# First 290 steps of a fused attention and mixer kernel in another order, with every copy of q and k on VectorE or ScalarE

## The chip, the core and the metric

The kernel runs on one core of a Trainium2 chip. The metric is device time in microseconds (us), from one launch to its end; the median of three runs is given. Engines are named as the profile names them: PE is TensorE (matrix products), DVE is VectorE, ACT is ScalarE, POOL is GpSimd, SP is SyncE. Each engine works through its own list of instructions strictly in order. It stops at an instruction whose inputs or whose output buffer another engine has not released yet, and everything behind it waits too.

## The reference, cut to what matters

Attention over 8 batches, 8 heads, 576 tokens and 64 numbers a head, with 16 extra "beacon" keys in front that every token may see; then a mixer over the 512 numbers of each token.

```python
k_all = np.concatenate([beacon_k, k], axis=2)
v_all = np.concatenate([beacon_v, v], axis=2)
scores = scale * np.matmul(q, k_all.transpose(0, 1, 3, 2))
scores = np.where(causal, -1000000000.0, scores)
a = np.exp(scores - scores.max(-1, keepdims=True))
a /= a.sum(-1, keepdims=True) + 1e-09
x = np.matmul(a, v_all)                  # then heads side by side: (8, 576, 512)
...
h = x.transpose(0, 2, 1) @ U @ V         # rank 32 over tokens
u = x + h.transpose(0, 2, 1)
out = u + np.maximum(u @ w_ch1, 0.0) @ w_ch2
```

## The kernel before

The work is cut into **pairs**: pair p holds two heads of one batch, so pairs 0 to 3 are batch 0, pairs 4 to 7 batch 1, and so on to 31. The mixer is cut into nine **blocks** of 512 rows. Nothing schedules itself: one long string, `SCRIPT` (from line 853), names the steps in the order in which they are written into all engines' lists. A step is a short name:

- `kqbv` and a batch: loads of k, q, beacon keys and v, issued from POOL (a letter A or B takes half of the heads). `w10` to `w13`, `w20`, `w21`: loads of the mixer's weights, from POOL too. `u`: small loads from SP for U and V. The first batch's q and k come ahead of the string, a pair at a time: pair 0's q from ACT's queue and everything else from SP's (k0, k1, q1, k2, q2, k3, q3, each a large transfer and a small one with the first 80 rows, "heads", tile `sth`).
- `GqA0`: the **regrouping** of q (or k) of pair 0 on engine A (ACT; V is DVE, G is POOL), from tile `stm` or `st` into `pr` (line 253). For batch 0 this is a cast from 32 to 16 bits, and a second cast brings the heads from `sth` to `hd` (line 741; `H` does that alone).
- `TqA0`: PE turns q of pair 0 (five transposes into the bank `tps`, lines 261 and 263), and engine A copies the result to `qT` or `kT` (two instructions: line 109 on ACT, lines 264 and 265 on DVE).
- `Sa0` to `Sd0`: the four **score visits** of pair 0: PE products `sps` (line 316), and two exponentials on ACT from `sps` to `expt` (line 321). `:3` puts three filler products ahead.
- `M0.0`: DVE masks the scores of one head (lines 304 and 306). `A0.0`: PE multiplies them with v (`po`, line 331), DVE divides by the sums (lines 339 and 340).
- `X0.0`, `X0.1`, `X0.2`: the mixer's rank-32 part for batch 0 (lines 371, 390, 397), with copies to `uT` on ACT (line 408) and DVE (line 406).
- `g0.9`: one of 16 first products of block 0 (four matmuls, line 529), with its relu on ACT (line 539), or ACT and DVE (lines 533 and 534). `p`, `P`: sums and second products of a block (lines 601, 620). `U`, `R`, `x`: transposes by DMA from SP's queue. `W`: sums of weights on DVE.
- `c`, `s`, `e`: three casts of the small loads (lines 163, 164), four copies on DVE (line 159), two products copied by ACT (line 170).
- `B` fills a tile for the masks on DVE. `I1` is a **filler**: one 128x512 product whose result nobody reads (line 241). It keeps PE at work while data are on their way.

There are two kinds of buffers that bind the order: eight PSUM banks, taken in turn by all products, and four score tiles (`expt_120` to `expt_123`), two for each pair, so that pair p+2 waits for pair p.

POOL's queue is served by a limited number of loads at a time: each load waits until the eighth one before it has landed.

Of the kernel before, what the change touches and what calls it, by code (L numbers as in the profile page):

```python
# [27 lines left out]
def kernel(  # L28
# [760 lines left out]
    def step(t):  # L789
# [65 lines left out]
        I1 Sb0 I1 I1 I1 TqV1 Sd0 q1A Sc0 I1 M0.0 GkV3 I1 I1 Sa1:2 I1 GqV2 I1 Sb1 M0.1 I1 I1 GkG2 I1 TkA2  # L855
        TqV2 TkA4 I1 q1B I1 w10 v0B w12 GqA4 I1 Sc1 A0.0 TkV3 Sd1 GqV3 I1 A0.1 Sd2 Sb2 Sa2:1 I1 Sc2 M1.1
        s M1.0 TqV3 GkG5 I1 A1.1 A1.0 Sc3 GqV6 Sa3:1 M2.1 I1 cG I1 I1 GqV5 k1B Sb3 TqV6 I1 Sd3 TqA4 w13
        M2.0 eA k2 M3.1 M3.0 I1 TqA5 A2.1 A2.0 Sc4 Sa4 TkV5 I1 A3.1 GqA7 I1 I1 A3.0 Sd5 Sc5 GkV7 TqV7
        X0.0 Sd4 GkA6 I1 X0.2 X0.1 I1 U0.0 Sa5:0 v1A Sb4 Sb5 g0.8 TkA7 GkV9 M5.1 M4.1 GkV11 M4.0 g0.1
        M5.0 g0.15 g0.0 b2 TkA6 U0.1 GkV8 g0.10 q2 A5.1 A5.0 Sb7 Sa7 Sd7 w11 A4.1 A4.0 g0.11 GqV9 g0.3  # L860
        Sc7 GqV8 M7.1 M7.0 g0.12 Sb6 Sd6 TqV8 TkV9 TkV11 TqV9 g0.2 Sa6:0 GqA11 Sc6 M6.0 v1B g0.14 g0.5
        M6.1 g0.6 g0.9 A6.0 A7.1 A7.0 TkA8 A6.1 w20 g0.13 p00.0 w21 g0.4 Sc9 Sd8 X1.0 g0.7 p01.0 X1.2
        X1.1 p01.1 P01.0 GkV10 p00.1 W0 Sd9 U1.1 TqA11 Sb9 Sa8 W4 W5 W1 P02.0 W2 W3 U0.2 v2 W6 P01.1
# [5 lines left out]
        Sc12 p11.0 GqV15 X2.0 M12.0 P11.0 GkA17 P11.1 U1.2 X2.1 GkV16 p11.1 R15 P12.0 P12.1 R16 P16.0
        TqV14 Sd13 Sb13 M12.1 p10.1 p10.2 Sc13 P16.1 b5 U2.2 M13.0 TkA14 v3 A12.1 q5 A12.0 R17 GkA19  # L870
        P15.0 P15.1 p11.2 Sa14 Sd14 Sc14 x12 P17.0 TkV15 M13.1 P13.0 U2.3 A13.0 Sb14 Z16 M14.0 P17.1
        P13.1 GqA19 GqA18 TkV16 TqA16 A13.1 g2.13 g2.10 TqV17 TqV15 M14.1 v4 g2.4 Sa15 k5 Sc15 TkA17
        P14.0 A14.0 P14.1 A14.1 Sd16 GqV20 Sb15 Sd15 M15.1 GkV18 g2.0 x14 Sc16 M15.0 g2.7 g2.5 g2.2
        A15.0 A15.1 x13 Sd17 Sb17 g2.9 U2.0 X3.0 b6 Sa16 X2.2 g2.3 x15 Sa17 Sb16 R18 R19 Z18 GkV20 M16.1
        Sc17 M17.1 M17.0 g2.1 g2.6 g2.12 M16.0 g2.8 g2.15 A17.0 U2.1 TqA19 GqA21 TqA18 X3.1 A16.1 A17.1
        g2.14 A16.0 X3.2 g2.11 p21.0 P21.0 P21.1 GqA23 GkA21 q6 TkA18 p20.0 P22.0 P22.1 TkA19 R20 p21.1
        p20.1 Sc18 Sb18 P26.0 P26.1 R21 Sc19 Sd18 Sa19 p21.2 P25.0 P25.1 GkV22 p20.2 I1 Sd19 Sa18 M18.0
        U3.0 Sb19 M19.0 P27.0 M18.1 M19.1 P23.0 GqV24 GqA22 TqV20 P27.1 x16 P23.1 g3.11 TqA21 GkV23
        TkV20 TkA21 R22 b7 A19.1 g3.7 A19.0 R23 g3.13 g3.8 g3.5 Sa21 Sb21 Sc21 P24.0 P24.1 A18.1 A18.0
        Sb20 U3.3 Sd21 Sa20 M21.1 M21.0 g3.3 g3.2 Sc20 Sd20 X4.0 g3.4 M20.0 k6 GkV24 M20.1 g3.15 GqA26  # L880
        N5 v5 TkV22 g3.12 A21.0 U3.1 A20.0 g3.10 N1 GkA26 g3.1 x17 q7 g3.0 A20.1 TqV22 TqA23 TkV23 g3.6
        g3.14 g3.9 p30.0 p30.2 A21.1 Sc23 GkV25 p31.0 Sb23 GqV25 Sa23 R24 p30.1 x18 P31.0 P31.1 GkV27
        P32.0 P32.1 TkA24 p31.1 Sc22 p31.2 U3.2 k7 Sd22 v6 Sa22 P36.0 P36.1 Sb22 x19 M22.1 Sd23 M23.0
        P35.0 R25 R26 M22.0 P35.1 X4.1 P37.0 P37.1 X4.2 GqV27 TqA24 TqA25 P33.0 U4.1 P33.1 TkA25 P34.0
        R27 g4.0 GqV28 A22.1 TkV26 GkA28 R28 M23.1 g4.11 GqV29 g4.2 g4.6 TqV26 A23.0 g4.10 A23.1 Sd25
        Sc25 A22.0 g4.4 GkV29 R29 Sb25 GkV30 Sa25 M25.0 Sd24 TqV27 P34.1 TkA27 g4.3 U4.3 TkV28 M25.1
        g4.15 g4.13 g4.9 Sc24 Sa24 x21 Sb24 M24.0 U4.2 X5.0 A25.0 M24.1 g4.8 g4.12 U4.0 GqV31 x22 g4.1
        p40.0 p40.1 GqA30 A25.1 g4.7 Sa27 Sb27 A24.1 g4.14 A24.0 g4.5 p41.0 GkV31 Sc27 x23 Sc26 p41.2
# [140 lines left out]
```

## Time and profile before

| | |
|---|---|
| median of three runs | 341.4 us (340.95 to 341.75) |
| the profiled execution | 341.91 us, its span from the first to the last instruction 340.3 us |
| instructions in it | 8963 |
| DVE, ACT, POOL busy | 263.4 us (77%), 228.3 us (67%), 103.6 us (30%) |
| moved by DMA | 44.17 MB, mean 130 GB/s |

The profile's first part gives busy time, share of the span and number of instructions of each engine. Its "windows" view gives the same for chosen stretches of time. In "lines" and "timeline" views a row names the line, engine and operation, the tile written and the tile read, shapes, then either `xcount | busy us, mean ns | idle before <- releaser`, or start, duration and, in brackets, how long the engine had been idle and what ended it.

### The profile page before, as it was taken

Reading aid. Unit: us, or ns where it says so; the run is one execution under the profiler, and the core shown is the slowest. Engines: PE = TensorE matmul, PEld = TensorE weight load, DVE = VectorE, ACT = ScalarE, POOL = GpSimd, SP = SyncE. Lnnn points to the kernel's source line nnn. Section 1 sums busy time; section 2 is a strip of 40 time slices with the busy share of each in tenths; the row PEclk is TensorE's granted clock in tenths of the full one; section 3 lists DMA queues with packets and bytes.
Section 4 is the critical chain, followed back from the end, with each engine's and each line's share of the span. In section 5 each row is a group of like instructions: output and inputs, shape, how many; then the busy total and the mean of one; then the engine's idle time right before and its main releaser. Section 6 shows DMA issues by size and latency. Waiting matters only on the chain.

```text
span 340.3 us, 8963 instructions
## 1 busy us (share of the span) xinstructions
PE 330.1 (97%) x3527; PEld 227.9 (67%) x3527; DVE 263.4 (77%) x681; ACT 228.3 (67%) x495; POOL 103.6 (30%) x137
## 2 busy tenths in 40 slices
...
GB/s 170 237 188 167 126 184 197 118 127 213 159 163 189 163 203 127 128 148 191 183 95 145 175 174 115 33 161 99 48 63 159 85 13 63 77 3 94 3 80 128
DMA packets 135600, 44.17 MB, mean 130 GB/s; under 512 B 108384, under 2 KB 130912, under 8 KB 135552
## 3 DMA queue, kind: packets, MB, share of 16 engines
...
## 4 chain that ended last, share of the span: by engine, by line
PE 84%; DVE 10%; issue 2%; ACT 1%; DMA 1%; ACTq 0%; DVEq 0%
PE gps L529 25%; PE cpY L620 17%; PE cpD L620 9%; PE sps L316 8%; PE po L331 8%; PE cpA L620 4%; PE fpY L566 3%; DVE gT L581 3%; PE idle L241 2%; PE tps L263 2%; PE fpD L566 2%; DVE sT L601 1%; DVE ob L645 1%; DMA sth<-in_beacon_k_dram 1%; PE ups L397 1%
## 5 line engine op out<-in xcount | busy, mean ns | idle before, releaser
L321 ACT ACTIVATE expt<-sps 128x496 f16<-128x496 f32 (+2 forms) x256 | 111.6, 543 | 13.4 <-PE sps L316 11.9
L529 PE MATMUL gps<-uT,w 128*128 128x512 f16 x384 | 91.8, 380 | 0.0
L620 PEld LDWEIGHTS <-gT 128*128 128x128 f16 x576 | 54.6, 98 | 10.5 <-issue 2.3
L529 PEld LDWEIGHTS <-w 128*128 128x128 f16 x384 | 34.3, 98 | 37.1 <-issue 2.4
L587 POOL TENSOR_SCALAR gT<-gT 128x512 f16<-128x512 f16 x12 | 17.8, 1493 | 105.7 <-DVE gT L581 89.1
L620 PEld LDWEIGHTS <-sT 128*128 128x128 f16 x432 | 40.8, 98 | 8.0 <-issue 2.0
L203 POOL DMA_DIRECT2D vs<-in_v_dram x50 | 40.8, 838 | 3.8 <-DMA w<-in_moe_w_ch_dram 1.7
L304 DVE TENSOR_TENSOR expt<-expt,bigmask 128x512 f16<-128x512 f16 x64 | 26.9, 421 | 18.8 <-ACT expt L321 18.8
L331 PEld LDWEIGHTS <-expt 128*128 128x128 f16 (+1 forms) x960 | 35.2, 98 | 8.7 <-DVE expt L304 1.1
L539 ACT ACTIVATE gT<-gps 128x512 f16<-128x512 f32 x48 | 29.3, 618 | 15.4 <-PE gps L529 14.9
L331 PE MATMUL po<-vs,expt 128*128 128x65 f16 (+1 forms) x960 | 37.8, 194 | 0.7 <-DVE expt L304 0.6
L620 PE MATMUL cpY<-wsum,gT 128*128 128x256 f16 x288 | 36.1, 273 | 0.0
L620 PE MATMUL cpD<-w,sT 128*128 128x256 f16 x288 | 35.6, 273 | 0.3 <-DVE sT L601 0.3
L316 PE MATMUL sps<-qT,kT 64*128 64x80 f16 (+4 forms) x384 | 34.3, 284 | 0.2 <-DVE qT L265 0.2
L340 DVE TENSOR_TENSOR xb<-po,rec 128x320 f16<-128x320 f32 x64 | 31.5, 492 | 2.2
L534 DVE SCALAR_TENSOR_TENSOR gT<-gps,gT 128x256 f16<-128x256 f32 x48 | 19.7, 420 | 13.0 <-ACT gT L533 12.9
L109 ACT ACTIVATE hP<-fpY 128x512 f32<-128x512 f32 x24 | 13.7, 597 | 23.1 <-PE fpY L566 22.0
L533 ACT ACTIVATE gT<-gps 128x256 f16<-128x256 f32 x48 | 18.9, 412 | 12.2 <-PE gps L529 11.9
L316 PEld LDWEIGHTS <-kT 64*128 64x128 f16 x384 | 13.8, 94 | 19.8 <-issue 11.1
L645 DVE TENSOR_TENSOR ob<-cpY,ut 128x512 f32<-128x512 f32 (+1 forms) x28 | 18.7, 667 | 5.9 <-PE cpY L620 5.9
L566 PEld LDWEIGHTS <-wf 128*128 128x128 f16 x192 | 18.6, 98 | 3.1 <-issue 0.7
L620 PE MATMUL cpY<-w,gT 128*128 128x256 f16 x144 | 17.7, 273 | 0.0
...
## 6 DMA issues: line engine op xcount, KB each, us to landing
...
w<-in_moe_w_ch_dram POOLq DMA_DIRECT2D x2, 1024.0 KB, 12.0
stm<-in_k_dram SPq DMA_DIRECT2D x4, 256.0 KB, 6.0
out_dram<-ob SPq DMA_DIRECT2D x4, 256.0 KB, 2.8
```

What stands on the lines that cost most here:

```text
L203: nc.gpsimd.dma_start(out=dst[a : a + nq[j], j, :, :], in_=src[hs, ds(q0[j], nq[j]), :].rearrange("h p d -> p h d"))
L304: nc.vector.tensor_tensor(out=e4, in0=e4, in1=bigmask, op=ALU.min)
L316: nc.tensor.matmul(ps[i][:, ds(o, w)], kT[hp, c, ds(P * ch, P)], qT[hp, c, ds(qa, w)], start=True, stop=True,)
L321: nc.scalar.activation(out=ex[i][:, ds(PAD + SLOT * g, gw[g])], in_=ps[i][:, 0 : gw[g]], func=AF.Exp, scale=scale)
L331: nc.tensor.matmul(po[:, j, :], ex[0 : nk[c], ds(blk[(c, j)], P)], vs[0 : nk[c], ds(c * H * E + h * E, E)], start=(c == 0), stop=(c == j),)
L340: nc.vector.tensor_tensor(out=xb[:, h // 2, :, ds(D * (h % 2), D)], in0=po[:, :, 0:D], in1=r.broadcast_to([P, NT, D]), op=ALU.mult)
L529: nc.tensor.matmul(g, w1[:, cc, ts(dc, P)], uT[:, cc, ds(ring(t0), 512)], start=(cc == 0), stop=(cc == NCC - 1))
L534: nc.vector.scalar_tensor_tensor(out=gT[:, dc, H2:512], in0=g[:, H2:512], scalar=0.0, in1=gT[:, dc, 0:H2], op0=ALU.max, op1=ALU.subtract,)
L539: nc.scalar.activation(out=gT[:, dc, :], in_=g, func=AF.Relu)
L566: nc.tensor.matmul(ps[:, i, :], a[:, kk, ts(2 * mp + i, P)], b[:, kk, :], start=opens and i == 0 and kk == 0, stop=kk == 1, skip_group_che ...
L620: nc.tensor.matmul(ps[:, i, :], a[:, f, ds(P * i, P)], b[:, f, :], start=opens and i == 0 and f == 0, stop=f == NK - 1, skip_group_check=True,
L645: nc.vector.tensor_tensor(out=out, in0=ps[:, ii, :], in1=other, op=ALU.add)
```

## The change

The change rewrites the first 290 of the string's 960 steps, up to `P04.0` before and `g1.8` after; from `U1.0` on the two strings are the same word for word. Line 853's string is all that differs. Two lines of the difference, at its start and at its end:

```diff
-        B I1 GqA0 HqA0 I1 I1 I1 k1A I1 b1 I1 HkV0 GkV0 TkV0 v0A TqA0 Sa0:3 I1 GqG1 u I1 GkV1 TkV1 GkA4
+        HqA0 I1 GkA0 I1 I1 I1 GqA0 I1 I1 HkV0 u I1 I1 I1 GkV1 I1 B I1 I1 I1 TqA0 TkA0 I1 TkV1 I1 s v0A
...
-        g1.5 P07.1 g1.3 A10.0 g1.0 TkV12 M11.0 M10.1 g1.6 g1.12 TqA12 GqV16 A11.1 g1.10 TkV13 P04.0 U1.0
+        g1.8 U1.0 U1.3 TqA13 GkA15 P04.1 g1.14 A11.0 k4 A10.1 Sa13 Sd12 g1.11 p10.0 g1.4 GqA17 g1.13
```

The same steps stand in the new order, but 29 of them name another engine. The four on POOL (`GqG1`, `GkG2`, `GkG5`, `cG`) become `GqV1`, `GkV2`, `GkA5`, `cV`. The others swap DVE and ACT: 12 regroupings or turns go from DVE to ACT (`GkA0`, `TkA0`, `TqA3`, `TkA5`, ...) and 13 from ACT to DVE (`TkV2`, `GqV4`, `TqV4`, `GkV4`, `TkV4`, `TqV5`, ...). POOL keeps only its loads. These are now v of batch 0 in both halves first, then q, k and weights of batch 1; before, half of k of batch 1 came first. The number of fillers is the same, 36 lone ones among the steps up to `X1.0` in both; 13 of them now stand ahead of the first turn, and 6 did before.

ACT's list at the opening, before and after. `hd_142` is the heads of q, `pr` the regrouped q or k, `qT` and `kT_124` the turned ones. Before:

```order
L109 ACTIVATE pr<-stm 128x512
L109 ACTIVATE hd_142<-sth 80x128
L109 ACTIVATE qT<-tps 128x64
L109 ACTIVATE qT<-tps 128x512
L321 ACTIVATE expt_120<-sps_225 128x496
L321 ACTIVATE expt_121<-sps_226 128x496
L109 ACTIVATE pr<-st_191 128x512
```

After:

```order
L109 ACTIVATE hd_142<-sth 80x128
L109 ACTIVATE pr<-stm 128x512 x2
L109 ACTIVATE qT<-tps 128x64
L109 ACTIVATE qT<-tps 128x512
L109 ACTIVATE kT_124<-tps 128x80
L109 ACTIVATE kT_124<-tps 128x512
L321 ACTIVATE expt_120<-sps_258 128x208
```

ACT now regroups and copies both q and k of pair 0 before its first exponential, and that one belongs to another visit, whose products stand on PE behind the turn of pair 1's k.

DVE's list where the casts of the small loads (lines 163 and 164) have come from POOL. `expt_121` is the second head's scores of pair 2, `po` the product with v. Before, around the mask of the same head:

```order
L340 TENSOR_TENSOR xb<-po,rec 128x5x64
L253 COPY pr<-st_192 128x512
L304 TENSOR_TENSOR expt_121<-expt_121,bigmask 128x4x128
L306 TENSOR_TENSOR expt_121<-expt_121,mask 80x80
L253 COPY pr<-st_192 128x512
```

After:

```order
L340 TENSOR_TENSOR xb<-po,rec 128x5x64
L163 CAST Usb<-small 128x128
L163 CAST Usb<-small 80x32
L164 CAST one<-small 32x576
L304 TENSOR_TENSOR expt_121<-expt_121,bigmask 128x4x128
L306 TENSOR_TENSOR expt_121<-expt_121,mask 80x80
L253 COPY pr<-st_429 128x512
```

Three casts now stand between pair 1's last division and the mask of pair 2, for which PE's next product with v waits.

ACT's list just ahead of the second batch's mixer part (line 408). Before:

```order
L321 ACTIVATE expt_122<-sps_1257 128x496
L321 ACTIVATE expt_123<-sps_1258 128x496
L321 ACTIVATE expt_120<-sps_1267 128x208
L321 ACTIVATE expt_121<-sps_1268 128x208
L533 ACTIVATE gT<-gps 128x256
L408 ACTIVATE uT<-ups 128x336 x2
```

After:

```order
L321 ACTIVATE expt_122<-sps_1232 128x496
L321 ACTIVATE expt_123<-sps_1233 128x496
L533 ACTIVATE gT<-gps 128x256
L321 ACTIVATE expt_120<-sps_1286 128x208
L321 ACTIVATE expt_121<-sps_1287 128x208
L533 ACTIVATE gT<-gps 128x256
L321 ACTIVATE expt_120<-sps_1299 128x496
L321 ACTIVATE expt_121<-sps_1300 128x496
L321 ACTIVATE expt_120<-sps_1309 128x496
L321 ACTIVATE expt_121<-sps_1310 128x496
L408 ACTIVATE uT<-ups 128x240 x2
```

Score visits have moved ahead of this point. Between the first batch's copies to `uT` and the second's, ACT has 26 exponentials before and 34 after (12 and 18 of them 128x496, 8 and 8 128x464, 6 and 8 128x208), 7 and 8 of the 128x256 relus, 8 and 8 of the 128x512 ones, and 7 and 8 copies (line 109).

More of the change, by code (lines that the diff above doesn't have):

```diff
@@ L853 @@
     SCRIPT = """
-        B I1 GqA0 HqA0 I1 I1 I1 k1A I1 b1 I1 HkV0 GkV0 TkV0 v0A TqA0 Sa0:3 I1 GqG1 u I1 GkV1 TkV1 GkA4
[L855 to L863, printed above, removed]
@@ L864 @@
-        GqA10 Sc8 Sb8 U0.3 M8.1 p00.2 M8.0 P02.1 TkA10 P05.0 Sa9 b3 p01.2 TqA10 P05.1 P06.0 P06.1 A8.0
-        b4 k3 GkA13 A8.1 Sa10 Sc10 M9.1 P03.0 P03.1 q3 q4 P07.0 A9.1 g1.9 g1.8 M9.0 A9.0 W7 Sb11 Sc11
-        g1.2 g1.7 Sb10 Sd10 M10.0 GqV12 GkV12 R12 g1.1 g1.15 GqA14 Sa11 GqV13 R13 GkA14 R14 Sd11 M11.1
-        g1.5 P07.1 g1.3 A10.0 g1.0 TkV12 M11.0 M10.1 g1.6 g1.12 TqA12 GqV16 A11.1 g1.10 TkV13 P04.0 U1.0
-        U1.3 TqA13 GkA15 P04.1 g1.14 A11.0 k4 A10.1 Sa13 Sd12 g1.11 p10.0 g1.4 GqA17 g1.13 Sa12 Sb12
@@ L869 @@
[L869 to L888, printed above, removed]
@@ L889 @@
-        p41.1 Sd26 P41.0 P41.1 Sa26 Sd27 M27.1 Sb26 P45.0 p40.2 P42.0 P42.1 P45.1 TkA29 x20 X5.1 U5.3
-        A27.1 R30 TqV29 M27.0 P46.0 P46.1 P43.0 P43.1 g5.13 A27.0 M26.0 M26.1 Sd29 g5.11 X5.2 g5.4 U5.1
-        TqV28 P47.0 g5.2 A26.1 TkA30 x27 P47.1 A26.0 N0 Sb29 Sc29 R31 N4 g5.6 N2 Sb28 Sa29 g5.0 x24
+        HqA0 I1 GkA0 I1 I1 I1 GqA0 I1 I1 HkV0 u I1 I1 I1 GkV1 I1 B I1 I1 I1 TqA0 TkA0 I1 TkV1 I1 s v0A
+        Sd0 Sb0 Sa0:3 I1 GqV1 TqV1 GkV2 Sc0 I1 GqV2 v0B I1 I1 Sc1 Sb1 I1 M0.0 Sd1 M0.1 TqV2 TkV2 I1 A0.0
@@ new lines @@
+        I1 GqV3 Sa1:2 A0.1 M1.0 Sd2 I1 GkV3 q1A M1.1 Sc2 TqA3 Sb2 I1 k1A Sa2:1 TkV3 I1 M2.0 I1 A1.0 I1
+        A1.1 Sd3 Sa3:1 w12 I1 Sb3 cV M2.1 GqV4 A2.1 b1 k1B TqV4 GkA5 Sc3 I1 GkV4 I1 M3.0 q1B eA GqV5
+        TkV4 I1 GkV7 TkA5 I1 w13 A2.0 Sd4 M3.1 I1 TqV5 A3.0 GkA6 b2 w10 I1 A3.1 k2 Sa4 I1 Sd5 GqV6 GqV7
+        TkA7 X0.0 X0.1 Sa5:0 X0.2 Sb4 TqV7 TqV6 Sc5 TkA6 v1A g0.9 Sc4 M4.1 Sb5 M5.1 U0.0 U0.2 g0.13
+        GkV11 g0.1 M5.0 g0.10 g0.0 GkV8 g0.14 q2 g0.3 g0.11 GkA9 A5.0 A5.1 Sb7 I1 w11 TkV8 GqV8 GqV9 Sa7
@@ new lines @@
+        g0.2 M4.0 GqV11 Sd7 Sc7 TkV11 TkA9 g0.8 A4.1 M7.0 TqA9 A4.0 p00.0 p00.1 Sb6 v1B Sa6:0 g0.12
+        p00.2 TqV11 M7.1 Sc6 g0.4 Sd6 g0.15 M6.0 GkA10 w20 U0.1 M6.1 TqV8 g0.6 A7.1 A7.0 Sd9 Sc9 w21
+        A6.1 g0.7 A6.0 Sd8 g0.5 Sc8 Sa8 GqV10 X1.0 v2 b3 p01.0 p01.2 X1.1 P02.0 p01.1 X1.2 W0 P01.0 Sb8
+        W4 W5 W1 Sb9 Sa9 W2 U1.1 W6 P01.1 TkA10 P02.1 M8.1 M9.0 TqA10 W7 b4 M8.0 U0.3 P05.0 P05.1 q3
+        P06.0 P06.1 M9.1 A8.1 A9.0 A8.0 Sa10 P03.0 P03.1 k3 g1.15 A9.1 q4 Sa11 Sd10 g1.5 g1.1 Sb10 Sc10
@@ new lines @@
+        g1.3 g1.2 GkV13 GqA12 M10.0 GkA12 W3 P07.0 M10.1 P07.1 GqA13 Sb11 Sd11 GqA14 Sc11 M11.1 g1.9
+        M11.0 GkA14 g1.12 A10.0 g1.7 g1.10 g1.0 R12 R13 R14 g1.6 TkV12 TqV12 TkV13 P04.0 GqA16 A11.1
+        g1.8 U1.0 U1.3 TqA13 GkA15 P04.1 g1.14 A11.0 k4 A10.1 Sa13 Sd12 g1.11 p10.0 g1.4 GqA17 g1.13
+        Sa12 Sb12 Sc12 p11.0 GqV15 X2.0 M12.0 P11.0 GkA17 P11.1 U1.2 X2.1 GkV16 p11.1 R15 P12.0 P12.1
+        R16 P16.0 TqV14 Sd13 Sb13 M12.1 p10.1 p10.2 Sc13 P16.1 b5 U2.2 M13.0 TkA14 v3 A12.1 q5 A12.0 R17
@@ new lines @@
+        GkA19 P15.0 P15.1 p11.2 Sa14 Sd14 Sc14 x12 P17.0 TkV15 M13.1 P13.0 U2.3 A13.0 Sb14 Z16 M14.0
+        P17.1 P13.1 GqA19 GqA18 TkV16 TqA16 A13.1 g2.13 g2.10 TqV17 TqV15 M14.1 v4 g2.4 Sa15 k5 Sc15
+        TkA17 P14.0 A14.0 P14.1 A14.1 Sd16 GqV20 Sb15 Sd15 M15.1 GkV18 g2.0 x14 Sc16 M15.0 g2.7 g2.5
+        g2.2 A15.0 A15.1 x13 Sd17 Sb17 g2.9 U2.0 X3.0 b6 Sa16 X2.2 g2.3 x15 Sa17 Sb16 R18 R19 Z18 GkV20
+        M16.1 Sc17 M17.1 M17.0 g2.1 g2.6 g2.12 M16.0 g2.8 g2.15 A17.0 U2.1 TqA19 GqA21 TqA18 X3.1 A16.1
@@ new lines @@
+        A17.1 g2.14 A16.0 X3.2 g2.11 p21.0 P21.0 P21.1 GqA23 GkA21 q6 TkA18 p20.0 P22.0 P22.1 TkA19 R20
+        p21.1 p20.1 Sc18 Sb18 P26.0 P26.1 R21 Sc19 Sd18 Sa19 p21.2 P25.0 P25.1 GkV22 p20.2 I1 Sd19 Sa18
+        M18.0 U3.0 Sb19 M19.0 P27.0 M18.1 M19.1 P23.0 GqV24 GqA22 TqV20 P27.1 x16 P23.1 g3.11 TqA21
+        GkV23 TkV20 TkA21 R22 b7 A19.1 g3.7 A19.0 R23 g3.13 g3.8 g3.5 Sa21 Sb21 Sc21 P24.0 P24.1 A18.1
+        A18.0 Sb20 U3.3 Sd21 Sa20 M21.1 M21.0 g3.3 g3.2 Sc20 Sd20 X4.0 g3.4 M20.0 k6 GkV24 M20.1 g3.15
@@ new lines @@
+        GqA26 N5 v5 TkV22 g3.12 A21.0 U3.1 A20.0 g3.10 N1 GkA26 g3.1 x17 q7 g3.0 A20.1 TqV22 TqA23 TkV23
+        g3.6 g3.14 g3.9 p30.0 p30.2 A21.1 Sc23 GkV25 p31.0 Sb23 GqV25 Sa23 R24 p30.1 x18 P31.0 P31.1
+        GkV27 P32.0 P32.1 TkA24 p31.1 Sc22 p31.2 U3.2 k7 Sd22 v6 Sa22 P36.0 P36.1 Sb22 x19 M22.1 Sd23
+        M23.0 P35.0 R25 R26 M22.0 P35.1 X4.1 P37.0 P37.1 X4.2 GqV27 TqA24 TqA25 P33.0 U4.1 P33.1 TkA25
+        P34.0 R27 g4.0 GqV28 A22.1 TkV26 GkA28 R28 M23.1 g4.11 GqV29 g4.2 g4.6 TqV26 A23.0 g4.10 A23.1
```

6 lines of the change are left out of this document (added).

## The prediction

> **What bounds the kernel now.** I read the page first: busy time, then the chain that ended last.
>
> ```profile
> span 340.3 us, 8963 instructions
> PE 330.1 (97%) x3527; PEld 227.9 (67%) x3527; DVE 263.4 (77%) x681; ACT 228.3 (67%) x495; POOL 103.6 (30%) x137
> PE 84%; DVE 10%; issue 2%; ACT 1%; DMA 1%; ACTq 0%; DVEq 0%
> ```
>
> PE is the bound, and the change gives it the same products as before. So the time can change only by the time in which PE waits or runs slowly, and only where the order changed. Next I cut the span at the opening's marks: the first filler, the first turn, the end of the slow products, the first and the second batch's copies to `uT`, and 115 us, by which the old order is back. Columns are the stretch, its length, then busy time and count for PE, PE's weight loads, DVE, ACT and POOL, the granted clock, DMA share and GB/s.
>
> ```profile
> 1.59:6.06 4.47, 2.74 (x6) 0.73 (x7) 0.96 (x10) 2.32 (x4) 4.46 (x10) 1.00 0.93 208
> 6.06:12.16 6.10, 6.02 (x27) 2.60 (x28) 2.44 (x8) 2.73 (x6) 3.82 (x7) 1.00 1.57 221
> 12.16:35.17 23.01, 21.94 (x307) 12.81 (x306) 18.33 (x60) 20.49 (x53) 18.09 (x28) 1.00 1.45 190
> 35.17:60.40 25.23, 25.23 (x308) 14.46 (x308) 18.67 (x59) 21.65 (x54) 14.60 (x19) 1.00 1.52 169
> 60.40:115.00 54.60, 54.58 (x605) 37.79 (x606) 43.56 (x112) 43.10 (x96) 19.49 (x25) 1.00 1.59 157
> 115.00:340.00 225.00, 219.55 (x2282) 159.47 (x2280) 178.78 (x423) 138.03 (x285) 42.26 (x44) 1.00 0.76 110
> ```
>
> From 35 to 115 us PE has no gap at all, so a wait put there is paid in full. In the two stretches between 12 and 60 us its helpers have little left: DVE is free for 4.68 us (23.01 less 18.33) and then 6.56, ACT for 2.52 and then 3.58. Between 60 and 115 us ACT is free for 11.5 us. The question is therefore whether the new order loads ACT and DVE more in the tight stretches.
>
> **The change, first the opening.** The timeline's rows of the first scores:
>
> ```profile
> 1.59 2.74 PE L241 MATMUL idle<-ident 128*128 128x512 f16 x6 [1.59 <-POOL ident masks.py:199]
> 7.28 1.49 PE L241 MATMUL sps<-ident 128*128 128x512 f16 x3
> 8.70 0.22 DVE L741 CAST hd<-sth 80x128 f16<-80x128 f32 x1 [0.52 <-DMA sth<-in_k_dram]
> 9.33 1.06 ACT L321 ACTIVATE expt<-sps 128x496 f16<-128x496 f32 x2 [1.09 <-PE sps L316]
> 10.06 0.27 PE L261 MATMUL tps<-ident,hd 80*128 80x80 f16 x1
> 10.13 0.63 PE L263 MATMUL tps<-ident,pr 128*128 128x128 f16 x4
> 10.55 0.63 PE L241 MATMUL idle<-ident 128*128 128x512 f16 x1
> 17.12 0.81 PE L241 MATMUL idle<-ident 128*128 128x512 f16 x3
> ```
>
> The 13 fillers that now come first end at 1.59 + 13 x 0.43 = 7.2 us at the slow rate (six took 2.74 with the tail of the last), so they cost at most 0.3 us against data that ACT has regrouped by about 6.7 (its old cast of q ends at 5.60, and one more cast and the heads follow). What decides is the next item: PE's first score visit now stands behind the turn of pair 1's k. Its heads are cast only when their transfer has landed, at 8.70, and nothing in the order moves that transfer. The turn can begin at about 8.95, takes 0.49 (10.06 to 10.55), a filler 0.43, the first products 0.4: the first exponential begins at about 10.25, not at 9.33. That is 0.9 us late on ACT. With PE at its later speed (three fillers in 0.81 in place of 1.49) it would be about 0.4. Bounds 0 to 0.9. ACT had gaps to give back, since it is busy for only 2.73 of 6.10 us there: I take **+0.6**.
>
> **The casts and copies that come to DVE.** Groups between 5 and 35 us, DVE's and then POOL's (count, busy, mean, idle before):
>
> ```profile
> L253 DVE CAST pr<-stm 128x512 f16<-128x512 f32 x5 | 2.2, 438 | 0.6 <-DMA stm<-in_k_dram 0.6
> L253 DVE COPY pr<-st 128x512 f16<-128x512 f16 x3 | 1.1, 374 | 0.0
> L265 DVE COPY qT<-tps 128x512 f16<-128x512 f16 x5 | 3.4, 678 | 0.0
> L264 DVE COPY qT<-tps 128x64 f16<-128x64 f16 x5 | 0.9, 188 | 1.8 <-PE tps L263 1.7
> ...
> L253 POOL CAST pr<-stm 128x512 f16<-128x512 f32 x2 | 1.2, 610 | 1.1 <-DMA stm<-in_q_dram 0.6 <-PE tps L263 0.5
> L163 POOL CAST Usb<-small 128x128 f16<-128x128 f32 (+1 forms) x2 | 0.7, 373 | 0.0
> L164 POOL CAST one<-small 32x576 f16<-32x576 f32 x1 | 0.7, 658 | 0.0
> ```
>
> Up to the first batch's mixer part DVE has one 32-bit regrouping more (6, not 5: 0.44), two casts of heads (0.22 each by the row above: 0.44), three 16-bit regroupings (6, not 3: 3 x 0.37 = 1.12), the three casts of the small loads, and one turn fewer (0.68 + 0.19 = 0.87). No trace shows the three casts on DVE: on POOL they take 1.40, and the 32-bit regrouping takes 0.44 on DVE against 0.61 on POOL, so I put them at 1.40 x 0.44 / 0.61 = 1.0. Together +2.1 us, against 4.68 free. By the sum it is hidden; by its place it is not. The three casts stand ahead of the mask of pair 2's second head, PE's next product with v waits for that mask, and behind it wait all of PE's later products. The wait exists already in small:
>
> ```profile
> 24.02 0.63 PE L331 MATMUL po<-vs,expt 128*128 128x65 f16 x15 [0.62 <-DVE expt L304]
> 20.53 1.16 DVE L741 CAST hd<-sth 80x128 f16<-80x128 f32 x1
> 20.66 1.02 DVE L339 RECIPROCAL rec<-po 128x5 f32<-128x5 f32 x1
> 20.00 0.82 POOL L203 DMA_DIRECT2D vs<-in_v_dram  x1 [0.42 <-DMA st<-in_q_dram]
> 20.81 0.76 POOL L180 DMA_DIRECT2D w<-in_moe_w_ch_dram  x1
> ```
>
> Bounds 0 (all hidden) to 2.1 (all seen). I take **+1.4**: the casts whole and a fifth of the rest, since this row shows PE already waiting for DVE here.
>
> The same rows hold an argument for the change: a cast of heads that takes 0.22 elsewhere took 1.16 beside POOL's work. [...] What POOL did at that moment was to issue two loads, by the rows above, and loads it still issues; I take nothing off.
>
> **ACT between the two batches' mixer parts.** ACT gets 34 exponentials there, not 26: six more of 128x496 and two of 128x208, one more 128x256 relu and one more regrouping. Means over the whole run:
>
> ```profile
> L321 ACT ACTIVATE expt<-sps 128x496 f16<-128x496 f32 x128 | 68.1, 611 | 5.3 <-PE sps L316 4.6 <-ACT kT L109 0.6
> L321 ACT ACTIVATE expt<-sps 128x208 f16<-128x208 f32 x64 | 19.4, 373 | 4.4 <-PE sps L316 4.2
> L533 ACT ACTIVATE gT<-gps 128x256 f16<-128x256 f32 x48 | 18.9, 412 | 12.2 <-PE gps L529 11.9
> L109 ACT ACTIVATE pr<-st 128x512 f16<-128x512 f16 x23 | 14.8, 652 | 4.3 <-DMA st<-in_k_dram 4.3
> ```
>
> That is 6 x 0.61 + 2 x 0.37 + 0.41 + 0.65 = 5.5 us more, so 27.1 us of work where it had 21.65 in 25.23. PE's own share of the moved steps is about four visits of 0.3 and one first product of 0.9, some 2.1 us, which PE no longer does later: for PE this is only displaced, and its stretch becomes 27.3. ACT would fit with no gap at all (0), or keep its old gaps of 3.58 us and end at 30.7, 3.4 us late. Bounds 0 to 3.4. Its gaps are short waits for PE between relus, copies and exponentials, and that alternation stays; and the exponentials stand ahead of the copies to `uT`, for which PE's first products of the next block wait. I take **+2.7**, nearer the upper end. What ACT saves after 60 us is worth nothing: it has 11.5 us free there, and PE none.
>
> Everything else I cost at nothing. The other swaps between DVE and ACT nearly cancel, POOL's copies leave an engine that PE hardly waits for, and after 115 us the order is the old one and PE works off the same list.
>
> **The sum**: 0.6 + 1.4 + 2.7 = 4.7 us. The profiled execution took 341.9 us (span 340.3), which becomes 346.6; it lies 0.5 above the median of the three runs, so the forecast is **346.1 us**. With all bounds it is 341.4 to 347.8.
>
> **Rivals.** *The opening at full speed* (faster). Thirteen fillers without a gap could bring PE to full speed before 8.95 us; in the run shown, PE stood still from 4.33 to 6.06 and was slow until about 12.2. From 8.95 to 12.16 it would need half, a gain of 1.6 us: 339.8, if both the DVE and the ACT term are at zero. It decides as long as scores, not landings, hold up the opening. For it: the filler rows, 0.43 each early and 0.22 or so later. Against it: ACT is full by the third window. [...] Chance 0.14.
>
> *All hidden*: DVE's and ACT's gaps close and PE never sees it: 341.5, chance 0.08.
>
> *The loads come late* (much slower). Half of k of batch 1 was POOL's first load; now twelve loads of v go ahead of q and k.
>
> ```profile
> 1.87 0.95 POOL L196 DMA_DIRECT2D st<-in_k_dram  x1
> L203 POOL DMA_DIRECT2D vs<-in_v_dram x15 | 11.1, 763 | 3.8 <-DMA w<-in_moe_w_ch_dram 1.7 <-DMA st<-in_k_dram 1.7 <-DMA st<-in_q_dram 0.4
> st<-in_q_dram POOLq DMA_DIRECT2D x2, 256.0 KB, 6.2
> ```
>
> Twelve issues of 0.76 and two waits put q's issue at 12 us and, with 6.2 us to land and a queue that is full, its landing at 18 to 20. DVE asks for it at about 26, so there are 6 us of cover. If that fails, DVE stands with masks behind it, and 3 to 4 us come on top: 349.5, chance 0.10.
>
> **How the numbers follow.** The forecast has 0.68, late loads 0.10, so slower has 0.78; about 0.2% (0.7 us) is what a measurement of this kernel can tell from no change, and *all hidden* is the 0.08 within it; faster has 0.14. The likeliest case alone spans 341.4 to 347.8. The range goes from 340.6, which takes in the weaker half of the faster case, to 349.5.
>
> **What would show it.** In the profile after: the first exponential at about 10.2 us; a wait of PE's line 331 for DVE's line 304 of a microsecond or more near 27; ACT over 95% busy from the first to the second copy to `uT`, and the second some 4 us later than 60.4; the window behind it with PE full and ACT freer than now. Wrong would be a PE without gaps up to 60 us, or a first exponential before 9.3.

## The result, and the profile after

| | before | after |
|---|---|---|
| median of six runs each | 341.57 us (340.95 to 342.43) | 339.72 us (339.42 to 340.20) |
| the profiled execution, its span | 341.91 us, 340.3 us | 340.20 us, 338.5 us |

The ratio is 0.9946, with a 95% interval of 0.9928 to 0.9964: faster by 1.85 us. The forecast was 346.1 us, slower; the range began at 340.6. The time is that of the rival *the opening at full speed* (339.8), which had been given 0.14.

From the page after, the busy time of each engine. PE's has fallen by 1.6 us and the span by 1.8.

```profile
PE 328.5 (97%) x3527; PEld 228.3 (67%) x3527; DVE 264.9 (78%) x690; ACT 227.9 (67%) x494; POOL 99.8 (29%) x129
```

The same stretches as in the prediction, after (length, then busy time and count of PE, weight loads, DVE, ACT, POOL; granted clock, DMA share, GB/s):

```profile
1.59:6.06 4.47, 4.47 (x11) 1.63 (x12) 0.07 (x3) 2.01 (x4) 4.34 (x9) 1.00 0.91 221
6.06:12.16 6.10, 5.63 (x52) 2.62 (x50) 4.43 (x21) 5.25 (x14) 5.20 (x8) 1.00 1.54 228
12.16:35.17 23.01, 21.08 (x305) 12.82 (x300) 19.98 (x70) 19.66 (x50) 14.20 (x21) 1.00 1.56 195
35.17:60.40 25.23, 25.23 (x302) 14.40 (x301) 19.43 (x61) 22.80 (x57) 14.20 (x18) 1.00 1.52 160
60.40:115.00 54.60, 54.27 (x603) 37.96 (x601) 42.92 (x108) 41.32 (x92) 20.70 (x27) 1.00 1.66 164
```

The second row is where most of the lead arises: between 6.06 and 12.16 us PE made 27 products in 6.02 busy us before and 52 in 5.63 now. ACT had 2.73 us of work done there and now has 5.25. The count matters here, since a slow PE also reads as a busy one. The opening itself, from the timelines of PE, DVE and ACT (start, duration, in brackets the idle time and what ended it):

```profile
1.59 5.50 PE L241 MATMUL idle<-ident 128*128 128x512 f16 x13 [1.59 <-POOL ident masks.py:199]
6.92 0.20 PE L261 MATMUL tps<-ident,hd 80*128 80x80 f16 x1
13.59 0.21 PE L261 MATMUL tps<-ident,hd 80*128 80x80 f16 x1 [0.60 <-DVE hd L741]
...
7.10 0.22 DVE L741 CAST hd<-sth 80x128 f16<-80x128 f32 x1
...
9.07 5.71 ACT L321 ACTIVATE expt<-sps 128x208 f16<-128x208 f32 x14 [0.35 <-PE sps L316]
```

The heads of pair 1's k, cast at 8.70 before, are cast at 7.10. PE is at full speed when the fillers end (a turn's first product takes 0.20; before, at 10.06 us, still 0.27), it stays so, and ACT gets 14 exponentials without a gap, the first at 9.07 against 9.33.

The first batch's copies to `uT` on ACT start at 31.80 (before 35.17). The second batch's stand level in both; the first row is before's, the others are after's:

```profile
60.42 1.37 ACT L408 ACTIVATE uT<-ups 128x336 f16<-128x336 f32 x4 [0.45 <-PE ups L397]
```

```profile
60.36 0.67 ACT L408 ACTIVATE uT<-ups 128x240 f16<-128x240 f32 x2
31.80:61.20 29.40, 29.40 (x358) 17.35 (x356) 23.00 (x70) 26.79 (x67) 15.06 (x20) 1.00 1.59 162
```

This stretch got longer, from 25.25 to 28.56 us, yet PE has no gap in it (29.40 of 29.40 us busy): it holds more of PE's work, which is missing elsewhere. The first products of the two mixer parts on PE, two rows before and two after, tell how much:

```profile
33.30 0.46 PE L371 MATMUL qtp<-xb,Usb 128*32 128x128 f16 x20
58.09 0.46 PE L371 MATMUL qtp<-xb,Usb 128*32 128x128 f16 x20
30.44 0.59 PE L371 MATMUL qtp<-xb,Usb 128*32 128x128 f16 x20
58.59 0.47 PE L371 MATMUL qtp<-xb,Usb 128*32 128x128 f16 x20
```

Between them PE begins 305 products in 24.79 us before and 338 in 28.15 after, without a gap in either. Counted by their columns, at the pace of 28 products of 512 columns in 6.05 us (from 36.05 on in the trace after), the difference is about 2.8 of the 3.4 us, an estimate. So the lead of 3.4 us at the first copies is worth less than it looks, and level at the second copies isn't a loss.

### The profile page after: what moved, and what is told of

Its sections match the earlier page's. It is cut to its first block, busy times and chain, and to the rows that moved or that the text cites. A ratio compares the mean times of both kernels' runs of the same rounds, so it can differ in the third digit from the quotient of the medians.

```text
span 338.5 us, 8950 instructions
## 1 busy us (share of the span) xinstructions
PE 328.5 (97%) x3527; PEld 228.3 (67%) x3527; DVE 264.9 (78%) x690; ACT 227.9 (67%) x494; POOL 99.8 (29%) x129
## 4 chain that ended last, share of the span: by engine, by line
PE 69%; DVE 17%; DMA 6%; issue 3%; ACT 2%; SPq 1%; DVEq 0%; ACTq 0%
PE gps L529 21%; PE cpY L620 14%; PE cpD L620 7%; PE po L331 7%; PE sps L316 7%; DMA stm<-in_q_dram 4%; PE cpA L620 3%; PE fpY L566 3%; DVE gT L581 3%; DMA raw<-pr 3%; DVE ob L645 2%; DVE sT L601 2%; DVE uT L404 2%; PE fpD L566 2%; DVE xb L340 1%
```

## The experiments

All kernels differ from before or after in the order string only. Each ratio is to the kernel before on the same chip, with its 95% interval; the medians of before were 341.5 to 342.1 us. A trace shows a single execution, which need not be a typical one: those of `b_fill`, `b_ord`, `a_nofill`, `a_actlate` and `a_cLate` took 0.7 to 1.6 us more than the median of their kernel, those of `b_both`, `b_three` and `a_hold` 0.7 to 2.8 us less. In the diffs, and below, **F** is 13 leading fillers in a row, **L** is v ahead of batch 1's k in POOL's queue, and **R** is pair 3's k cast behind pair 2's q.

### One part of the change alone, put into the kernel before

F alone, `b_fill`:

```diff
- ... HkV0 GkV0 TkV0 ... Sa0:3 I1 GqG1 u I1 GkV1 ... I1 Sb0 I1 I1 I1 TqV1 ... Sc0 I1 M0.0
+ ... HkV0 GkV0 I1 I1 I1 I1 I1 I1 I1 TkV0 ... Sa0:3 GqG1 u GkV1 ... Sb0 TqV1 ... Sc0 M0.0
```

> The kernel before with one part of the change alone: 13 fillers in a row ahead of the first turn (before: 6), the same 36 in all; loads, engines and every other step stay. Theory F (the gap-free row of fillers brings PE to full speed early and this is the gain): the fillers become fast by about 6.9 us instead of PE being slow until 12.2, PE's products from 9 to 12.2 take half, 1.0 to 1.6 us faster than before, as far as the landings of pair 1's k and q (8.7 and 10.3 us) let it. Theory L (earlier landings of the first batch's q and k make the gain): within 0.3 us of before. My forecast's opening term: no gain, up to 0.3 us slower.

Measured: 341.93 us, 0.9991 (0.9975 to 1.0006). The fillers did bring the full speed by 6.1 us, and nothing was gained. PE's timeline, of the longest of the twelve executions (342.65 us), shows why, and the windows below it show the granted clock (the column of 0.50 and 0.65):

```profile
1.58 4.72 PE L241 MATMUL idle<-ident 128*128 128x512 f16 x13 [1.58 <-POOL ident masks.py:199]
9.39 0.21 PE L261 MATMUL tps<-ident,hd 80*128 80x80 f16 x1 [1.21 <-DVE hd L741]
11.99 0.25 PE L261 MATMUL tps<-ident,hd 80*128 80x80 f16 x1 [1.86 <-POOL hd L741]
12.03 0.63 PE L263 MATMUL tps<-ident,pr 128*128 128x128 f16 x4
```

```profile
12.00:14.00 2.00, 2.00 (x15) 1.11 (x16) 0.79 (x2) 1.02 (x4) 2.00 (x4) 0.50 1.25 295
14.00:16.00 2.00, 2.00 (x7) 0.37 (x5) 0.53 (x2) 0.87 (x3) 2.00 (x4) 0.65 1.59 213
```

A fast PE stands still for heads that have not landed (1.21 and 1.86 us), and then its clock is at half for over 2 us: the four products of a turn take 0.63 again, not 0.39.

L alone, `b_load` (with pair 4's regrouping four steps later):

```diff
- ... k1A I1 b1 I1 HkV0 GkV0 TkV0 v0A TqA0 ... TkV1 GkA4 I1 Sb0 ... Sc0 I1
+ ... v0A I1 I1 HkV0 GkV0 TkV0 k1A b1 TqA0 ... TkV1 I1 Sb0 ... Sc0 GkA4 I1
```

> The kernel before with only POOL's first loads swapped: half of v of batch 0 goes ahead of half of k of batch 1 and its beacon keys (with the regrouping of pair 4's k put four steps later on ACT so that it need not wait). Theory L: the first batch's transfers from SP's queue land earlier (heads of pair 1's k at about 7.1 us instead of 8.7, q of pair 1 at 8.0 instead of 10.3) and the kernel gains 0.7 to 1.5 us. Theory F: the landings may move, but PE stays slow until about 12 us, and at most 0.5 us is gained. My forecast (nothing in the order moves that transfer): the landing stays within 0.2 us of 8.7 and the time too.

Measured: 341.00 us, 0.9973 (0.9956 to 0.9990). The heads of pair 1's k landed at 7.28 and pair 1's q at 8.29 us, against 8.68 and 10.32 before. So the order of POOL's loads does move SP's transfers. Alone it brought half of the change's gain: the heads of pair 1's k were cast by 8.36 us (before 8.92), yet PE's turn of them reached DVE at 10.77 (before 10.79).

R alone, `b_ord`:

```diff
- ... M0.0 GkV3 I1 I1 Sa1:2 I1 GqV2 I1 Sb1 M0.1 I1 I1
+ ... M0.0 I1 I1 Sa1:2 I1 GqV2 I1 Sb1 M0.1 GkV3 I1 I1
```

> The kernel before with the third part alone: the cast of pair 3's k behind that of pair 2's q and both masks of pair 0. Theory R with the two other conditions missing: PE is slow to 12 us and pair 2's transfers land late, so at most 0.5 us is gained. Rival (the order of casts makes the gain by itself): 1.0 to 1.9 us.

Measured: 341.29 us, 0.9979 (0.9961 to 0.9997).

### One part taken out of the change

`a_nofill` (without F):

```diff
- ... HkV0 u I1 I1 I1 GkV1 I1 B I1 I1 I1 TqA0 ... Sa0:3 I1 GqV1 TqV1 GkV2 Sc0 I1 GqV2
+ ... HkV0 u GkV1 B TqA0 ... Sa0:3 I1 I1 I1 GqV1 TqV1 GkV2 Sc0 I1 I1 I1 GqV2 I1 I1 I1
```

> The changed kernel with 7 of its 13 leading fillers put back behind the first visits, so that 6 stand ahead of the first turn as before. Theory F: PE is slow again until 10 to 12 us and the kernel loses 1.0 to 2 us against the change, which ends at about the time of before (341 to 342). Theory L: the landings stay early, it loses at most 0.4 us.

Measured: 341.87 us, 0.9994 (0.9978 to 1.0011). The whole gain is gone; in the trace a turn's first product still takes 0.27 us at 7.83, and 0.20 only at 12.70.

`a_k1first` (without L):

```diff
- ... GqA0 I1 I1 HkV0 ... TqA3 Sb2 I1 k1A Sa2:1 ... A2.1 b1 k1B
+ ... GqA0 k1A I1 b1 I1 HkV0 ... TqA3 Sb2 I1 Sa2:1 ... A2.1 k1B
```

> The changed kernel with half of k of batch 1 and its beacon keys again as POOL's first loads, ahead of v. Theory L: heads of pair 1's k land at about 8.7 us again instead of 7.1, the first exponential comes at about 10.2 (what my forecast had), and the kernel loses 1 to 2 us against the change. Theory F: PE is at full speed by 7 us and makes up for it, the loss is at most 0.6 us.

Measured: 342.21 us, 0.9997 (0.9979 to 1.0016). The opening is now the one that the forecast had:

```profile
10.12 2.43 ACT L321 ACTIVATE expt<-sps 128x208 f16<-128x208 f32 x6 [1.48 <-PE sps L316]
```

The forecast put this exponential at 10.25. But the loss can't be laid to k alone: the products with v waited 0.47, 0.69 and 0.90 us for their transfers at 15.67, 16.65 and 17.85, a wait that the change does not have. Together that is 2.06 us, as much as the whole gain.

`a_k3early` (without R):

```diff
- ... GkV2 Sc0 I1 GqV2 v0B ... Sd2 I1 GkV3 q1A
+ ... GkV2 Sc0 I1 GkV3 GqV2 v0B ... Sd2 I1 q1A
```

> The changed kernel with the cast of pair 3's k put ahead of that of pair 2's q on DVE, as before the change. Theory R: DVE waits for the landing of pair 3's k (14.3 us in the change), PE then for the turn of pair 2's q (13.59 in the change) until about 15.2, and 1.0 to 1.6 us are lost. Rival O: the score visits between are enough cover, at most 0.4 us is lost.

Measured: 343.12 us, 1.0045 (1.0028 to 1.0063). One cast moved, and 3.4 us are lost against the change by the ratios, twice what was expected: PE's wait is 2.25 us, and its clock drops behind it.

```profile
15.05 0.21 PE L261 MATMUL tps<-ident,hd 80*128 80x80 f16 x1 [2.25 <-DVE hd L741]
18.28 1.01 PE L331 MATMUL po<-vs,expt 128*128 128x65 f16 x15
```

```profile
14.00:16.00 2.00, 0.94 (x18) 0.83 (x19) 1.95 (x10) 0.57 (x3) 1.14 (x2) 1.00 1.81 180
16.00:18.00 2.00, 2.00 (x19) 0.74 (x15) 1.97 (x6) 0.00 (x0) 1.64 (x3) 0.54 1.55 206
```

### Parts together, in the kernel before

`b_both` is F with L, `b_lr` L with R, `b_three` all three; `b_three2` is `b_three` again, on the chip of `b_lr`.

> The kernel before with both parts together: 13 leading fillers in a row and half of v of batch 0 ahead of half of k of batch 1 in POOL's queue. Theory C (the two parts need each other: the fillers bring the full clock, the early landings leave PE no gap in which it falls back): PE fast from about 6.5 us on with gaps under 1 us, the waits and slow time up to the first mixer part fall by 2 to 3 us, and the kernel is 1.5 to 2.5 us faster than before, as fast as the change or faster, with POOL's copies and all other steps as before. Rival A (the parts only add): 0.9 us, what the swap of loads gave alone. Rival O (the rest of the new order makes the gain): at most 1 us.

> The kernel before with 13 leading fillers, v ahead of k of batch 1 on POOL's queue, and a third part of the change: the cast of pair 3's k on DVE moved behind that of pair 2's q and both masks of pair 0. With the first two alone PE waited 1.63 us at 15.76 for the heads of pair 2's q, whose cast stood on DVE behind that of pair 3's k, which lands last. Theory R (casts in the order in which the transfers land are the third condition): that wait falls below 0.4 us and 1.0 to 1.5 us more is gained, 339.5 to 340.2, level with the change. Rival O (other parts of the new order make the rest of the gain): the wait only moves to the next step, less than 0.4 us is gained against the 341.3 of the two parts alone.

> The kernel before with the swap of POOL's first loads and the later cast of pair 3's k, and without the 13 leading fillers (6 stand ahead of the first turn). Theory C (all three conditions are needed): PE is slow until about 11 us and the kernel stays at 0.997 to 0.999 of before. Rival A (the parts add and the fillers are worth nothing in the old order): 0.9952, the sum of 0.27% and 0.21% that the two gave alone, level with all three together.

> The kernel before with all three parts, again, on the same chip as the run without the fillers: 0.9955 by the first time, 0.9935 to 0.9975 by its interval. The difference to the run without the fillers is what the fillers are worth in the old order: 0.7 us or more by theory C, under 0.3 us by rival A.

Measured: `b_both` 341.32 us, 0.9980 (0.9964 to 0.9995); `b_three` 340.19, 0.9955 (0.9935 to 0.9975), and again 340.79, 0.9979 (0.9964 to 0.9995); `b_lr` 341.17, 0.9986 (0.9973 to 1.0000). So the new order loses its whole gain, or more, without any one of the three parts, but in the old one they bring 0.2 to 0.45%, and what each adds to the others is too near the scatter to be told. In `b_both` PE waited 1.63 us for pair 2's q behind pair 3's k, as read; in `b_three` that wait is gone. What held `b_three2` back is a wait that my own edit made. Its ACT and its PE:

```profile
14.34 0.63 ACT L109 ACTIVATE pr<-st 128x512 f16<-128x512 f16 x1 [2.61 <-DMA st<-in_k_dram]
...
15.49 0.20 PE L261 MATMUL tps<-ident,hd 80*128 80x80 f16 x1 [1.97 <-ACT expt L321]
```

With L, batch 1's k lands at 14.3 us; its regrouping `GkA4`, moved only four steps, stops ACT for it, exponentials stand behind it, and PE behind those (0.81 us of ACT in the first `b_three`). The change has no regrouping of batch 1 on any engine before 23.49 us. Whether this is all that the old order lacks wasn't tried.

### What the change adds on DVE and ACT

`a_cG` puts the three casts of the small loads back on POOL (`cV` to `cG`); `a_cLate` keeps them on DVE, three steps later (`Sb3 cV M2.1 GqV4 A2.1` to `Sb3 M2.1 GqV4 A2.1 cV`). First the place in the change itself:

```profile
22.21 0.62 DVE L163 CAST Usb<-small 128x128 f16<-128x128 f32 x2
22.43 0.70 DVE L164 CAST one<-small 32x576 f16<-32x576 f32 x1
23.05 0.40 DVE L304 TENSOR_TENSOR expt<-expt,bigmask 128x512 f16<-128x512 f16 x1
...
23.51 0.63 PE L331 MATMUL po<-vs,expt 128*128 128x65 f16 x15 [1.23 <-DVE expt L304]
```

> The changed kernel with the three casts of the small loads back on POOL at the same step. The forecast's DVE term (1.4 us, of which the casts whole, 1.0): 1.0 to 1.4 us faster than the change. By the trace of the change, where the casts take DVE from 22.21 to 23.05 and PE waits 1.23 us for the mask behind them: 0.5 to 0.8 us faster up to the first mixer part, if that lead survives to the end; the profile shows PE's wait at 0.3 to 0.6. Rival: the wait is another's (exponentials on ACT, which end at about 22.3), and it stays above 0.9 us with no gain.

> The changed kernel with the three casts still on DVE, three steps later: behind the mask of pair 2's second head, the regrouping of q of pair 4 and the last division of pair 2's second head. If place alone makes the cost, as much is gained as with the casts on POOL (0.5 to 0.8 us, PE's wait at 0.3 to 0.6); if the work on DVE makes it, the wait turns up at the next mask and the time stays within 0.2 us of the change.

Measured: `a_cG` 339.49 us, 0.9925 (0.9904 to 0.9946), PE's wait 0.43; `a_cLate` 339.63, 0.9924 (0.9901 to 0.9948), PE's wait 0.43, and then 0.69 at 24.83 for the cast itself. Against 339.72 and 339.91 for the change, the casts on DVE cost 0.1 to 0.4 us by the medians and 0.7 by the ratios (0.9945 and 0.9946 for the change), within the intervals either way. The casts hold DVE for 0.84 us in this trace, but for 0.58 in those of `a_same` and `a_hq1`, where PE's wait at the same place is 0.98 and 0.92.

`a_actlate` moves three score visits back behind the second batch's mixer part:

```diff
- ... A6.0 Sd8 g0.5 Sc8 Sa8 GqV10 X1.0 ... X1.2 W0 P01.0 Sb8
+ ... A6.0 g0.5 GqV10 X1.0 ... X1.2 Sd8 Sc8 Sa8 W0 P01.0 Sb8
```

> The changed kernel with three score visits (six exponentials, 3.2 of the 5.5 us that the change put on ACT there) moved back behind the second batch's mixer part. The forecast's ACT term (2.7 us for 5.5 us of work) makes this 1.6 us faster than the change. By the trace, in which PE's waits in this stretch are 0.9 us against 0.6 before, the work is hidden: within 0.3 us of the change.

Measured: 341.21 us, 0.9986 (0.9968 to 1.0005): 1.5 us slower, where the forecast's term said 1.6 faster. ACT now idles ahead of the copies to `uT` and then has eleven exponentials in a row, behind which PE's score products take 1.47 us for six, where six take 0.78 in the change. That is 0.7 of the loss; another 0.4 us is a wait near 93 us (0.46 for ACT's copy to `qT`, then 0.27), where the change waits 0.33:

```profile
59.17 0.63 ACT L408 ACTIVATE uT<-ups 128x240 f16<-128x240 f32 x2 [1.22 <-PE ups L397]
61.70 4.77 ACT L321 ACTIVATE expt<-sps 128x208 f16<-128x208 f32 x11
...
63.14 1.47 PE L316 MATMUL sps<-qT,kT 64*128 64x464 f16 x6
```

### Why SP's transfers land earlier

`a_hold`: a copy of one number on POOL, ahead of its first load, waits for pair 1's k (`s v0A` to `s Yk1 v0A`).

> The changed kernel with one tiny copy on POOL ahead of its first load, which waits until pair 1's k has landed, so that nothing of POOL's is in flight beside the first transfers of SP's queue. If these are slowed by what POOL's queue has in flight at the same time: pair 1's k lands before 6.3 us (6.67 in the change, 7.59 before) and pair 1's q before 7.8 (8.02). If the order within SP's own queue alone sets the landing: within 0.2 us of 6.67 and 8.02. Either way v of batch 0 comes some 4 us later and PE should wait for it at its first product with v (14.35 in the change), 0.5 to 3 us slower than the change.

Measured: 344.57 us, 1.0071 (1.0047 to 1.0094). Pair 1's k landed at 6.45 us (6.67 in the change and 6.74 in its second trace, `a_same`; expected was before 6.3 or no move), its q at 7.21 (8.02 and 8.04), pair 2's k at 8.74 (11.72 and 10.21). So the first transfer hardly moved and the later ones did. PE waited 0.88, 0.85 and 0.65 us for v from 14.68 on, as expected. The loss, 4.3 us by the ratios, is more than the 3 expected: the eight times go from 341.82 to 345.04, the trace is of the first of these, and what the others lost has no trace. The queues' rows of the first 8 us, packets, MB and share of 16 engines (q1 is SP's queue, q0 POOL's), before, after, and with the hold, where POOL has no row:

```profile
q1 hardware_dynamic: 917, 0.68, 37.3%
q0 software_dynamic: 817, 0.29, 33.6%
```

```profile
q0 software_dynamic: 1562, 0.19, 37.9%
q1 hardware_dynamic: 1212, 0.88, 40.9%
```

```profile
q1 hardware_dynamic: 1618, 1.17, 54.9%
```

The less POOL's queue moves early, the more SP's does, in these three traces: 0.68, 0.88 and 1.17 MB. v ahead of k puts 0.19 MB through POOL's queue in these 8 us instead of 0.29, in nearly twice as many packets.

`a_cG_hk2`, `a_cG_hq1` and `a_hq1` hold only the second half of v, until pair 2's k or pair 1's q has landed; the first two have the casts on POOL, too. `a_same` is the change on their chip.

> The changed kernel with the casts of the small loads on POOL and one tiny copy on POOL ahead of the second half of v, which waits until pair 2's k has landed. Theory (what POOL's queue has in flight slows SP's transfers, and these pace the opening): pair 2's k lands at 9.5 to 10.3 us (10.32 with the casts on POOL alone) and pair 2's q before 11.5 (12.27), ACT's gap of about 1.2 us near 16 shrinks below 0.5, PE's waits up to the first mixer part fall from 4.8 to 4.0 or less, and the kernel gains 0.5 to 1.2 us against 339.5. Rival: q and k of batch 1, which come 2 to 3 us later by this, reach DVE too late near 24 us, and the gain is eaten or more. Second rival: ACT's exponentials pace the opening, not the landings; within 0.3 us of 339.5.

> The same with the copy waiting for pair 1's q (8.2 us) in place of pair 2's k: the second half of v starts some 1.6 us later instead of 3.5. Theory: pair 2's q before 11.9 us, a gain of 0.2 to 0.7 us against 339.5. Rivals as before: at most 0.2 us, or a loss if batch 1's q is late.

> The changed kernel with only the copy on POOL that holds the second half of v until pair 1's q has landed, and the casts of the small loads on DVE as in the change. If the hold alone makes the gain of the version that had both (338.8): 339.0 to 339.3. If it needs the casts off DVE: 339.6 to 340.0, as the change, with PE's wait of about 1 us for the mask near 23 still there.

> The changed kernel itself, on the same chip as the two others. By its first runs 339.7 us; if the casts on POOL are worth the 0.5 to 0.8 us that the wait on PE shows, the kernel with them there (339.5 on another chip) is faster than this by that much only if nothing later takes the lead back; the 0.2 us between the two medians so far says that most of it is taken back near 90 us, where the transposes by DMA end no earlier.

Measured: `a_cG_hk2` 340.36 us, 0.9959 (0.9935 to 0.9984); `a_cG_hq1` **338.84**, 0.9918 (0.9896 to 0.9940); `a_hq1` 339.25, 0.9930 (0.9913 to 0.9948); `a_same` 339.91, 0.9945 (0.9924 to 0.9965). The expectation for `a_hq1` held (339.0 to 339.3 if the hold alone makes the gain). The expectation of earlier landings failed: pair 2's k landed at 10.79, 10.33 and 10.11 us in the three, against 10.21 in `a_same`. Only pair 3's transfers came earlier, its q at 14.95, 14.45 and 14.04 us, against 15.12; whether that makes the gain was not tried. In `a_cG_hk2` the late loads of batch 1 cost PE a wait of 0.80 us at 25.30 (`hd<-in_beacon_k_dram`). The version with the short hold and the casts on POOL is the fastest measured, 1.1 us below the change on the same chip, though the two intervals overlap. A part of that lies near 90 us, where the change gives back some of its lead. SP issues three transposes by DMA there, and DVE's copy to `kT` needs the first of them. Before, after and `a_cG_hq1`, from the timelines of SP, DVE and PE:

```profile
82.95 6.45 SPq L283 DMA_TRANSPOSE raw<-pr  x3
...
89.24 0.70 DVE L291 COPY kT<-raw 128x512 f16<-128x512 f16 x1 [0.82 <-DMA raw<-pr]
```

```profile
80.22 8.69 SPq L283 DMA_TRANSPOSE raw<-pr  x3
...
89.20 0.61 DVE L291 COPY kT<-raw 128x512 f16<-128x512 f16 x1 [1.56 <-DMA raw<-pr]
...
92.38 2.75 PE L529 MATMUL gps<-uT,w 128*128 128x512 f16 x12 [0.33 <-DVE ob L645]
```

```profile
78.65 7.38 SPq L283 DMA_TRANSPOSE raw<-pr  x3
...
86.28 0.83 DVE L291 COPY kT<-raw 128x512 f16<-128x512 f16 x1 [0.21 <-DMA raw<-pr]
```

The change issues them 2.7 us earlier and has the first copy only 0.04 us earlier, since the first of them takes 9.0 us to land and not 6.3. With a hold of POOL the three took 7.38 to 7.86 us, in the other kernels with the new order 6.86 to 8.69 (the long ones where they were issued early), and 5.50 to 6.49 in before and all kernels with the old order, in `b_three` too, which issued them at 80.73. Why is not settled.

## Why the prediction was wrong, step by step

**What bounds the kernel.** Right: PE is busy 97% in both, and the time changed only where PE waited or ran slowly. Most of that lies in the first 33 us, but not all: `b_ord` leads before by 0.8 us at the first mixer part and ends 0.5 us behind it, in its trace, and `a_same` has a lead of 0.9 us over the first trace of the change there and none at the end.

**The opening, +0.6.** The step that failed reads "nothing in the order moves that transfer". The order of POOL's loads moves it, by 1.4 us in `b_load`. With it went the exponential at 10.25, which came at 9.07. With the old loads (`a_k1first`) it came at 10.12, near the forecast, but partly by luck: the turn began 0.3 us later than forecast, at 9.24, and from there PE, at full speed, needed 0.9 us and not 1.3. The term's sign was wrong for a second reason: fillers were priced as time on PE (at most 0.3 us) and not as what they do to PE's speed, though that stood in the prediction as a rival.

**The rival that had the time** was right in its number, 339.8, and only half right in its mechanism; the match of the number is partly luck, since it set the DVE term at zero and the earlier loads were no part of it. Thirteen fillers bring full speed (in `b_fill` a turn's first product takes 0.20 us at 6.14), but alone they gain nothing: PE then idles for landings, 1.21 and 1.86 us, and its clock falls to 0.50. The rival's own condition, "as long as scores, not landings, hold up the opening", is what the earlier loads and the casts in the order of landing provide; that is the reading of the three runs that take one part out, of which `a_k1first` also delays v.

**Casts on DVE, +1.4.** The mechanism was right, place and releaser too: PE's wait for the mask, 0.62 before, is 1.23. The term was mis-sized. It took the casts whole (1.0) and a fifth of the rest. The casts hold DVE from 22.21 to 23.05, 0.84; without them 0.43 of the wait stays (`a_cG`). So it measured 0.8 at its place here, 0.5 to 0.6 in the traces of `a_hq1` and `a_same`, and 0.1 to 0.7 at the end, which is within the scatter.

The argument for the change that was named and not used is only partly borne out. The casts of heads, with POOL's copies gone and its loads left, take 244 ns in the mean in the change, none over 0.41 (0.55 once in `a_hq1`), where one took 1.16 before; in `b_load`, with POOL's copies back, one takes 1.08.

```profile
L741 DVE CAST hd<-sth 80x128 f16<-80x128 f32 x7 | 1.7, 244 | 4.5 <-DMA sth<-in_beacon_k_dram 4.5
```

But in before and in `b_load` POOL's copy starts only 0.14 and 0.06 us before the long cast ends, and until then POOL issues loads, as the prediction said; what lengthened these two stays open. In `b_both` a cast of heads of 0.92 us (8.49 to 9.41) does span a cast on POOL (8.69 to 9.32). That is one cast in one trace; whether POOL's cast lengthened it is not shown.

**ACT between the mixer parts, +2.7.** Wrong, and the largest error. The step "or keep its old gaps of 3.58 us", with the value taken near it, assumed that ACT's gaps are fixed. ACT's work rose to 26.79 in 29.40 us (91%, not over 95%), and its gaps shrank to 2.6 us there. PE has no gap between the two mixer parts, before or after, and of the 3.4 us by which the way from one to the other grew some 2.8 are work moved there, by the estimate above; about 0.6 us is left for ACT where the forecast had 2.7. The forecast's share of moved work, 2.1 us, was small too. The windows show none of the 0.9 and 0.6 us of waits that the expectation of `a_actlate` names. Moving three visits back cost 1.4 to 1.5 us, so having them early is a gain in this order.

**Late loads.** q of batch 1 landed at 18.83, inside the forecast's 18 to 20, and was asked at 23.49; the cover held, as the forecast had it, though DVE asked 2.5 us before the 26 that it reckoned with. With the second half of v held until 10.96 us (`a_cG_hk2`) q still landed in time, at 19.60; the beacon keys of batch 1, at 25.25, did not.

**The signs named.** A wait of a microsecond at line 331: yes, at 23.51. ACT over 95%, the second copies 4 us late: no. A PE without gaps to 60 us or an exponential before 9.3 was to mean wrong; the exponential came at 9.07. Of PE's lead of 2.9 us at the first mixer part (30.44 against 33.30), 1.7 are left at the end. Some 0.7 of it is no lead: PE has made 283 products by then after and 297 before, and the 14 come later (an estimate by their columns, as above). At the third batch's mixer part, with 1019 products made in both, the lead is 1.5 us (95.78 against 97.32). A wait of 0.33 us at 92.38 is new; for the rest no single wait was found.
